# Transposing Q with the DMA crossbar instead of TensorE in a fused attention and FFN kernel

## The chip, the cores and the metric

The kernel runs on one core of one Trainium2 chip. The metric is the device time of one execution in microseconds. A profile is one such execution recorded by the hardware profiler; its times count from the start of its span. Engines are called as the profile calls them: PE is TensorE (PEld its weight loads), DVE is VectorE, ACT is ScalarE, POOL is GpSimd and SP is SyncE, whose queue issues DMAs.

## What is computed

Sliding-window causal attention over 8 batches, 8 heads, 576 positions and 64 values per head, followed by a multiplicative feed-forward block on the 4608 tokens:

```python
scores = scale * np.matmul(q, k.transpose(0, 1, 3, 2))
rel = pos[:, None] - pos[None, :]
mask = (rel >= 0) & (rel < 64)
scores = np.where(mask, scores, -1000000000.0)
attn = np.exp(scores - np.max(scores, axis=-1, keepdims=True))
attn = attn / (np.sum(attn, axis=-1, keepdims=True) + 1e-09)
x = np.matmul(attn, v)              # then heads side by side: 4608 x 512
a, b = x @ w1, x @ w2               # 512 x 1024 each
h = a * b @ w3                      # 1024 x 1024
out = h @ w_out                     # 1024 x 512
```

Inputs and output are float32; the kernel computes in fp16 with float32 sums.

## The kernel before

**Attention.** Work goes in 48 steps `d`, six for each batch: three segments of queries (`SEGS`, 192 queries each) times two pairs of head pairs. Two heads share the 128 partitions (64 each, called `a`), and `j` counts the four pairs of heads. `scores(d)` multiplies a block of 128 keys (stationary, `kT`) with up to 128 queries (moving, `qT`), so that keys lie on the partitions of `s_ps`, eight matmuls in a step (line 278). One exponential on ScalarE (line 282) takes the step from PSUM to the fp16 tile `pt`, and GpSimd masks it in place with `affine_select` (lines 290 and 292; two for a step with two full blocks, four for the first segment, whose blocks have 128 and 64 queries). `values(d)` multiplies with V, whose added columns of ones give the sums; ScalarE takes logarithms and the exponential of their negative (lines 320 to 323), and DVE writes the normalised result to `xT` (lines 326 and 327).

**K and Q on their way.** `load_qk` brings a batch of K or Q from memory in two DMAs of 576 KB into a tile `stage` (four buffers). Partition p holds 18 consecutive positions of one head pair (`TP, TI = 32, 18`). `cast_qk` makes fp16 of it in `k16` or `q16` (one buffer each), mostly on GpSimd (line 214). `transposes` turns it on TensorE, 18 transposes of 128x128 in three groups of six into PSUM (line 253), and three copies (line 257: K all on DVE, Q two on DVE and one on ScalarE) put it into `kT` or `qT` in the order of positions.

**The feed-forward block.** w3 and w_out are multiplied together once, at the start. `ffn_ab(g, fc)` makes one of eight blocks of the product for 512 tokens with 16 matmuls (or eight per half; line 395), `ffn_o(g, t)` one of four blocks of 128 rows of the output with eight (line 408), and `store` sends it off from the SP queue.

**Order.** The order on each engine is that of the program text; nothing is scheduled automatically. Batches 0 and 1 are written out by hand, up to about 80 us. From batch 2 on, `tick(u)` counts twelve ticks to a batch: an even tick starts `scores(u // 2)`, an odd one does `values` of the step before, so that the values of step d come three ticks after its scores. The table `late` (line 335) tells in which tick of a batch the loads, casts and transposes for the coming batches are put. The list `slots` (line 608) deals out the feed-forward pieces between ticks. A waiting instruction holds up all behind it on its engine, or, on SP, all DMAs behind it. In tick 24, the first of batch 2, the masks of step 12 are followed on GpSimd by a cast of Q of batch 3, in tick 25 by the second cast, and in tick 26 by the masks of step 13.

Of the kernel before, what the change touches and what calls it, by code (L numbers as in the profile page):

```python
# [8 lines left out]
FP32 = mybir.dt.float32  # L9
FP16 = mybir.dt.float16  # L10
I32 = mybir.dt.int32
ALU = mybir.AluOpType
AF = mybir.ActivationFunctionType
PSUM = bass.MemoryType.PSUM

P = 128
SHIFT = 4.0
# [127 lines left out]
def kernel(  # L145
# [11 lines left out]
    nc = tc.nc  # L157
    B, H, S, D = q.shape
# [3 lines left out]
    scale = 1.0 / (D ** 0.5)  # L162
    NJ = H // 2
    TP, TI = 32, 18
    GT = 512
    NG = N // GT
    RING = 4 * S
# [12 lines left out]
    const = fast.enter_context(tc.tile_pool(name="const", bufs=1))  # L180
    sb = fast.enter_context(tc.tile_pool(name="sb", bufs=2))
    ps_t = fast.enter_context(tc.tile_pool(name="ps_t", bufs=1, space=PSUM))
    ps_s = fast.enter_context(tc.tile_pool(name="ps_s", bufs=1, space=PSUM))
# [3 lines left out]
    pool_cp = nc.gpsimd.tensor_copy  # L187
# [9 lines left out]

    raws, k16s, q16s = {}, {}, {}

    def load_qk(b, which, gate=None):  # L200
        src = k if which == "k" else q
        t = sb.tile([P, 2, TI * D], FP32, name="stage", bufs=4)
        if gate is not None:
            gate(t[:, 0, 0:1], 0.0)
        for hh in range(2):
            nc.sync.dma_start(out=t[:, hh], in_=src[b, hh:H:2].rearrange("j (p r) d -> p j (r d)", r=TI))
        raws[which, b] = t

    def cast_qk(b, which, hh, cp):
        t = raws[which, b]  # L210
        if hh == 0:
            (k16s if which == "k" else q16s)[b] = sb.tile([P, TI, P], FP16, name=which + "16", bufs=1)
        t16 = (k16s if which == "k" else q16s)[b]
        cp(t16[:, :, hh * D:hh * D + D], t[:, hh].rearrange("p (i d) -> p i d", d=D))

    def cast_third(b, which, c, cp):
        t = raws[which, b]
# [9 lines left out]
    def load_v(b, *blocks):  # L227

        vh = v_heads(b)
        for c in blocks:  # L230
            lo = D if c == 4 else 0
            s0 = VBLK[c] + lo
            nc.gpsimd.dma_start(out=vh[lo:P, c], in_=v[b, :, s0:s0 + P - lo, :].rearrange("h s d -> s h d"))  # L233

    def copy_v(b, c):
        vh = v_heads(b)
        dve_cp(vh[0:D, c], vh[D:P, c - 1])
        if c == 1:
            dve_cp(vh[D:P, 1], vh[0:D, 2])


    kTs, qTs = {}, {}

    def transposes(b, which, *cs, into=None, cps=None):

        t16, dst = (k16s, kTs) if which == "k" else (q16s, qTs)
        if cs[0] == 0:
            dst[b] = sb.tile([P, NJ, S], FP16, name=which + "T")
        if into is None:
            into = [ps_t.tile([P, 6, P], FP16, name="tp")]  # L250
        for c, tp in zip(cs, into):
            for i in range(6):
                nc.tensor.transpose(tp[:, i, :], t16[b][:, 6 * c + i, :], ident16)  # L253
        if cps is None:
            cps = [dve_cp if which == "k" or c != 1 else act_cp for c in cs]
        for c, tp, cp in zip(cs, into, cps):
            cp(dst[b].rearrange("q j (p i) -> q j p i", i=TI)[:, :, :, 6 * c:6 * c + 6],  # L257
               tp.rearrange("q i (p j) -> q j p i", p=TP))


    MASKS = [[(0, 1, 128, 0, 0), (128, 1, 64, 64, 0)]] + 2 * [[(0, 2, 128, 64, -64)]]
    probs, lns = {}, {}

    def scores(d):

        b, r = divmod(d, 6)
        si, jp = divmod(r, 2)
        kT, qT = kTs[b], qTs[b]
        seg = SEGS[si]
        w = sum(blk[2] for blk in seg)  # L270
        s_ps = ps_s.tile([P, 2, 2, 256], FP32, name="s_ps")
        for jj in range(2):
            j = 2 * jp + jj
            c0 = 0
            for (k0, q0, n, _) in seg:
                for a in range(2):
                    half = slice(a * D, a * D + D)
                    nc.tensor.matmul(s_ps[:, a, jj, c0:c0 + n], kT[half, j, k0:k0 + P], qT[half, j, q0:q0 + n],  # L278
                                     start=True, stop=True, skip_group_check=True)
                c0 += n  # L280
        pt = sb.tile([P, 2, 2, 256], FP16, name="pt", bufs=3)
        nc.scalar.activation(pt[:, :, :, 0:w], s_ps[:, :, :, 0:w], AF.Exp, bias=-SHIFT, scale=scale)  # L282

        rows = pt.rearrange("k a j n -> k (a j) n")
        for (lo, nb, n, off, step) in MASKS[si]:
            sl = rows[:, :, lo:lo + nb * n]
            pat = [[0, 4], [step, nb], [1, n]]
            if nb == 1:
                pat = [[0, 4], [1, n]]
            nc.gpsimd.affine_select(out=sl, in_=sl, pattern=pat, compare_op=ALU.is_ge,  # L290
                                    fill=0.0, base=off, channel_multiplier=-1)
            nc.gpsimd.affine_select(out=sl, in_=sl, pattern=[[-s, m] for s, m in pat], compare_op=ALU.is_ge,  # L292
                                    fill=0.0, base=63 - off, channel_multiplier=1)
        probs[d] = pt
# [34 lines left out]
    def keep_sums(n):  # L329
# [2 lines left out]
        nc.sync.dma_start(out=lnsum[2 * n:2 * n + 2, :], in_=y[0:P:D].rearrange("a j n -> a (j n)"))  # L332


    late = {0: [("t", 1, "k", 0), ("cast", 1, "q", 0)], 1: [("cast", 1, "q", 1)],
            2: [("t", 1, "k", 1), ("load", 2, "k")], 4: [("t", 1, "k", 2), ("v", 1, 0, 2, 3)],
            5: [("load", 2, "q")], 6: [("t", 1, "q", 0), ("v", 1, 4, 5)], 7: [("cast", 2, "k", 0)],
            8: [("t", 1, "q", 1), ("copy", 1, 4)], 9: [("copy", 1, 1), ("cast", 2, "k", 1)], 10: [("t", 1, "q", 2)]}

    def event(b, kind, ahead, *a):  # L340
        if b + ahead >= B:
            return
        if kind == "load":
            load_qk(b + ahead, *a)
        elif kind == "cast":
            cast_qk(b + ahead, *a, pool_cp)
        elif kind == "t":
            transposes(b + ahead, *a)
        elif kind == "v":
            load_v(b + ahead, *a)  # L350
        else:
            copy_v(b + ahead, *a)
# [25 lines left out]

    def ffn_ab(g, fc, nf=1, lo=0, hi=GT):

        if g not in abs_:
            abs_[g] = sb.tile([P, 8, GT], FP16, name="ab", bufs=3)
        ab = abs_[g]
        n = hi - lo
        a_ps = ps_f.tile([P, GT], FP32, name="f_ps")
        b_ps = ps_f.tile([P, GT], FP32, name="f_ps")
        x0 = (g * GT + lo) % RING
        cuts = [(0, n)] if x0 + n <= RING else [(0, RING - x0), (RING - x0, n)]
        for w, d in ((w1_sb, a_ps), (w2_sb, b_ps)):
            first = True  # L390
            for f in range(nf):
                for dc in range(4):
                    for c0, c1 in cuts:
                        xc = (x0 + c0) % RING
                        nc.tensor.matmul(d[:, f * n + c0:f * n + c1], w[:, dc, (fc + f) * P:(fc + f + 1) * P],  # L395
                                         xT[:, dc, xc:xc + c1 - c0], start=first, stop=(dc == 3),
                                         skip_group_check=True)
                        first = False
        a_sb = sb.tile([P, GT], FP32, name="a_sb", bufs=3)
        act_cp(a_sb[:, 0:nf * n], a_ps[:, 0:nf * n])  # L400
        nc.vector.tensor_tensor(ab[:, fc:fc + nf, lo:hi], b_ps[:, 0:nf * n].rearrange("p (f n) -> p f n", f=nf),  # L401
                                a_sb[:, 0:nf * n].rearrange("p (f n) -> p f n", f=nf), ALU.mult)
# [11 lines left out]
    def store():  # L414
        while stores:
            r0, o_sb = stores.pop()
            nc.sync.dma_start(out=out[r0:r0 + P, :], in_=o_sb)
# [39 lines left out]
    rows = 2 * 3 * B  # L457
# [48 lines left out]
    def spare(pool, name):  # L506

        t = pool.tile([P, 2, 1024], FP16, name=name)
        return [t[:, i, 0:768].rearrange("p (i n) -> p i n", i=6) for i in range(2)]
# [67 lines left out]
    for d in range(6, 11):  # L577
        values(d)
        if d < 10:
            scores(d + 2)  # L580
        for _ in range(2 if d in (6, 8) else 1):
            steps.pop(0)()
            store()
        if d == 6:
            load_v(2, 4, 5)
            copy_v(1, 4)
            load_qk(3, "k")
        else:
            which, hh = [("k", 0), ("k", 1), ("q", 0), ("q", 1)][d - 7]
            cast_qk(2, which, hh, pool_cp)  # L590
    transposes(2, "k", 0, 1, into=spare(ps_s, "s_ps"))
    values(11)
    transposes(2, "k", 2)
# [1 line left out]
        cast_qk(3, "k", hh, pool_cp)  # L595
    ffn_o(0, 3)
    store()
    transposes(2, "q", 0, 1, into=spare(ps_s, "s_ps"))
    transposes(2, "q", 2)
    copy_v(2, 1)  # L600
    copy_v(2, 4)
    load_qk(3, "q")
# [6 lines left out]
    for g in range(1, NG):  # L609
        part = [lambda g=g, fc=fc: ffn_ab(g, fc) for fc in range(8)] + \  # L610
               [lambda g=g, t=t: ffn_o(g, t) for t in range(4)]
        lo = need[g]
        hi = need[g + 1] if g + 1 < NG else NU
        for i, w in enumerate(part):
            ahead = (LAG + 1) * (min(1, (i + 1) / 4) if g == 1 else 1)
# [55 lines left out]
```

## Time and profile before

Three runs took 295.75, 296.19 and 296.27 us; the median is 296.19. The profiled execution has a span of 294.3 us.

| engine | busy us | share of the span | what it does most |
|---|---|---|---|
| PE | 274.1 | 93% | feed-forward matmuls, 134.1 + 67.1 us |
| DVE | 185.4 | 63% | products and copies out of PSUM |
| POOL | 180.8 | 61% | masks, 52.1 + 52.4 us; casts of K and Q, 28.3 us |
| ACT | 168.4 | 57% | exponentials 45.5 us, copies 41.7 us |

The groups of the page that touch the change, each with its number of instructions, its busy time and the mean duration of one:

| group | count | busy us | mean ns |
|---|---|---|---|
| score matmuls, 128 columns (line 278) | 320 | 17.8 | 219 |
| score matmuls, 64 columns | 64 | 4.4 | 189 |
| transposes of Q into `tp` (line 253) | 108 | 9.1 | 220 |
| copies of transposed Q on DVE, from `tp` (line 257) | 13 | 12.3 | 949 |
| copies of transposed Q on ACT, from `tp` | 5 | 4.0 | 808 |
| exponential of 1024 elements (line 282) | 32 | 32.6 | 1018 |
| exponential of 768 elements | 16 | 13.0 | 810 |
| casts of Q on POOL (line 214) | 13 | 14.6 | 1146 |

Matmuls overlap each other, so the mean of a matmul is longer than the time that it adds to TensorE's stream; that is read from the distance between starts of groups in the timeline. In the chain of work that ended last, PE has 76% of the span.

### The profile page before, as it was taken

Reading aid. Unit: us, or ns where it says so; the run is one execution under the profiler, and the core shown is the slowest. Engines: PE = TensorE matmul, PEld = TensorE weight load, DVE = VectorE, ACT = ScalarE, POOL = GpSimd, SP = SyncE. Lnnn points to the kernel's source line nnn. Section 1 sums busy time; section 2 is a strip of 40 time slices with the busy share of each in tenths; the row PEclk is TensorE's granted clock in tenths of the full one; section 3 lists DMA queues with packets and bytes.
Section 4 is the critical chain, followed back from the end, with each engine's and each line's share of the span. In section 5 each row is a group of like instructions: output and inputs, shape, how many; then the busy total and the mean of one; then the engine's idle time right before and its main releaser. Section 6 shows DMA issues by size and latency. Waiting matters only on the chain.

```text
span 294.3 us, 5925 instructions
## 1 busy us (share of the span) xinstructions
PE 274.1 (93%) x2254; PEld 152.9 (52%) x2254; DVE 185.4 (63%) x289; ACT 168.4 (57%) x281; POOL 180.8 (61%) x214
## 2 busy tenths in 40 slices
PE   7758889898799999999999999999999999999992
PEld 7544555444455555555555787555555445444440
DVE  0715688465787667687777866677867555554541
ACT  2513774676458647766686565487568866642300
POOL 8835995478749856696869463786595344402200
PEclk9999999999999999999999999999999999999998
DMA  6999999990277939094929470950094021012012
GB/s 231 219 181 201 265 278 212 373 131 36 74 266 264 72 110 321 39 85 143 322 20 100 136 295 2 155 73 1 20 171 40 0 74 72 0 38 109 0 57 95
DMA packets 51665, 38.85 MB, mean 132 GB/s; under 512 B 38784, under 2 KB 41856, under 8 KB 51632
## 3 DMA queue, kind: packets, MB, share of 16 engines
q0 software_dynamic: 41744, 9.96, 36.2%
q1 hardware_dynamic: 9888, 28.46, 26.6%
q8 instruction: 19, 0.31, 0.4%
q14 instruction: 14, 0.11, 0.1%
HBM read 38.80 MB, written 9.44 MB: 164 GB/s over the span
## 4 chain that ended last, share of the span: by engine, by line
PE 76%; DVE 6%; ACT 5%; DMA 4%; issue 3%; POOL 3%; POOLq 0%; DVEq 0%; ACTq 0%
PE f_ps L395 38%; PE f_ps L408 19%; PE o_ps L311 7%; PE tp L253 5%; DMA ab<-in_moe_w_dram 4%; PE s_ps L278 4%; DVE xT L327 2%; PE f_ps L454 2%; ACT ln_s L321 2%; ACT r L323 2%; POOL v L488 2%; DVE kT L257 1%; DVE xT L326 1%; ACT ln_s L320 1%; ACT pt L282 1%
## 5 line engine op out<-in xcount | busy, mean ns | idle before, releaser
L395 PE MATMUL f_ps<-xT,w_sb 128*128 128x512 f16 (+1 forms) x640 | 134.1, 358 | 0.0
L290 POOL TENSOR_SCALAR_AFFINE_SELECT pt<-pt 128x512 f16<-128x512 f16 (+1 forms) x64 | 52.1, 814 | 69.0 <-ACT pt L282 68.9
L395 PEld LDWEIGHTS <-w_sb 128*128 128x128 f16 x640 | 59.7, 98 | 50.7 <-issue 0.5
L408 PE MATMUL f_ps<-wc_sb,ab 128*128 128x512 f16 x288 | 67.1, 379 | 0.1
L401 DVE TENSOR_TENSOR ab<-f_ps,a_sb 128x512 f16<-128x512 f32 x72 | 49.8, 692 | 18.4 <-PE f_ps L395 15.8
L326 DVE TENSOR_TENSOR xT<-o_ps,r 64x384 f16<-64x384 f32 x48 | 26.4, 550 | 53.8 <-ACT r L323 53.6
L282 ACT ACTIVATE pt<-s_ps 128x1024 f16<-128x1024 f32 (+1 forms) x48 | 45.5, 949 | 18.0 <-PE s_ps L278 16.5
L400 ACT COPY a_sb<-f_ps 128x512 f32<-128x512 f32 x72 | 41.7, 579 | 24.8 <-PE f_ps L395 23.9
L292 POOL TENSOR_SCALAR_AFFINE_SELECT pt<-pt 128x512 f16<-128x512 f16 (+1 forms) x64 | 52.4, 819 | 4.4
L320 ACT ACTIVATE ln_s<-o_ps 64x384 f32<-64x384 f32 x48 | 23.4, 487 | 53.4 <-PE o_ps L311 53.3
L408 PEld LDWEIGHTS <-ab 128*128 128x128 f16 x288 | 26.9, 98 | 28.8 <-DVE ab L401 0.6
L233 POOL DMA_DIRECT2D v<-in_v_dram x40 | 33.9, 854 | 5.9 <-DMA ab<-in_moe_w_out_dram 4.1
L311 PE MATMUL o_ps<-pt,v 128*128 128x128 f16 (+1 forms) x384 | 27.9, 215 | 5.9 <-DVE xT L327 4.0
L311 PEld LDWEIGHTS <-v 128*128 128x128 f16 x384 | 23.5, 98 | 18.2 <-issue 3.5
L410 DVE COPY t2k<-f_ps 128x512 f32<-128x512 f32 x36 | 24.7, 690 | 11.6 <-PE f_ps L408 11.1
L327 DVE TENSOR_TENSOR xT<-o_ps,r 64x384 f16<-64x384 f32 x48 | 26.9, 561 | 0.6
L323 ACT ACTIVATE r<-ln_s 128x384 f32<-128x384 f32 x48 | 25.1, 523 | 1.5
L321 ACT ACTIVATE ln_s<-o_ps 64x384 f32<-64x384 f32 x48 | 23.1, 482 | 0.5
L278 PEld LDWEIGHTS <-kT 64*128 64x128 f16 x384 | 10.5, 94 | 16.5 <-issue 14.8
L278 PE MATMUL s_ps<-qT,kT 64*128 64x128 f16 (+1 forms) x384 | 18.2, 214 | 0.3 <-ACT pt L282 0.2
L257 DVE COPY kT<-tp 128x768 f16<-128x768 f16 x17 | 16.2, 952 | 0.1
L454 PE MATMUL f_ps<-ab,t2k 128*128 128x512 f16 x64 | 15.0, 379 | 0.4 <-DVE t2k L448 0.3
(59 smaller groups left out, 179.8 us busy)
## 6 DMA issues: line engine op xcount, KB each, us to landing
stage<-in_k_dram SPq DMA_DIRECT2D x16, 576.0 KB
stage<-in_q_dram SPq DMA_DIRECT2D x16, 576.0 KB
out_dram<-t2k SPq DMA_DIRECT2D x36, 256.0 KB
v<-in_v_dram POOLq DMA_DIRECT2D x32, 128.0 KB, 4.7
w_sb<-in_moe_w_dram POOLq DMA_DIRECT2D x4, 512.0 KB, 9.5
ab<-in_moe_w_out_dram POOLq DMA_DIRECT2D x1, 1024.0 KB, 10.6
ab<-in_moe_w_dram POOLq DMA_DIRECT2D x2, 512.0 KB, 12.6
xT<-in_moe_w_dram POOLq DMA_DIRECT2D x2, 512.0 KB, 16.2
```

The costliest lines, as they stand in the source:

```text
L233: nc.gpsimd.dma_start(out=vh[lo:P, c], in_=v[b, :, s0:s0 + P - lo, :].rearrange("h s d -> s h d"))
L278: nc.tensor.matmul(s_ps[:, a, jj, c0:c0 + n], kT[half, j, k0:k0 + P], qT[half, j, q0:q0 + n], start=True, stop=True, skip_group_check=True)
L282: nc.scalar.activation(pt[:, :, :, 0:w], s_ps[:, :, :, 0:w], AF.Exp, bias=-SHIFT, scale=scale)
L290: nc.gpsimd.affine_select(out=sl, in_=sl, pattern=pat, compare_op=ALU.is_ge, fill=0.0, base=off, channel_multiplier=-1)
L292: nc.gpsimd.affine_select(out=sl, in_=sl, pattern=[[-s, m] for s, m in pat], compare_op=ALU.is_ge, fill=0.0, base=63 - off, channel_multip ...
L311: nc.tensor.matmul(o_ps[:, jj, o0:o0 + n], v16[:, si * 2 + bi, j0 + jj, a * D:a * D + P], pt[:, a, jj, c0:c0 + n], start=first, stop=(bi = ...
L323: nc.scalar.activation(r, y, AF.Exp, scale=-1.0)
L327: nc.vector.tensor_tensor(xs[D:P], o_ps[D:P, :, 192:384], r[D:P], ALU.mult)
L395: nc.tensor.matmul(d[:, f * n + c0:f * n + c1], w[:, dc, (fc + f) * P:(fc + f + 1) * P], xT[:, dc, xc:xc + c1 - c0], start=first, stop=(dc ...
L400: act_cp(a_sb[:, 0:nf * n], a_ps[:, 0:nf * n])
L401: nc.vector.tensor_tensor(ab[:, fc:fc + nf, lo:hi], b_ps[:, 0:nf * n].rearrange("p (f n) -> p f n", f=nf), a_sb[:, 0:nf * n].rearrange("p ...
L408: nc.tensor.matmul(o_ps, ab[:, fc, t * P:t * P + P], wc_sb[:, fc, :], start=(fc == 0), stop=(fc == 7))
```

## The change

From batch 2 on (`FIRST = 2`) Q isn't transposed on TensorE any more. SP issues one DMA transpose for each batch (`turn`), which goes from `q16` in SBUF to a tile `q_tr` in SBUF, with no PSUM and no copy in between. It is meant to take the transposes off TensorE and the copies off DVE and ScalarE.

A partition now holds 16 consecutive positions (`QI`), so a batch's tile has 512 of the 576 positions. The last 64 of all batches and heads are loaded together as one more tile, `"last"`, cast and transposed once into `qlast`. `q_tr` has the order (position within 16, group of 16): the score matmuls read it as it lies, in runs of eight groups, and their result in PSUM has the same order. The exponential reads PSUM with a stride and writes `pt` in the order of positions, so all that follows is as it was. In the first segment it becomes two instructions. A block that crosses position 512 takes two matmuls in place of one. `stage` has three buffers instead of four.

```diff
+    def turn(b):
+        tr = qlast if b == "last" else sb.tile([P, QI, P], FP16, name="q_tr", bufs=2)
+        nc.sync.dma_start_transpose(tr, q16s[b].rearrange("q i n -> q (i n)"))
+        qTs[b] = tr
...
-        t = sb.tile([P, 2, TI * D], FP32, name="stage", bufs=4)
+        t = sb.tile([P, 2, TI * D], FP32, name="stage", bufs=3)
...
+            elif b == "last":
+                rows = q.rearrange("b (j e) s d -> e (b j) s d", e=2)[hh, :, TP * QI:S]
+                nc.sync.dma_start(out=t[:, hh, 0:QI * D], in_=rows.rearrange("j (p r) d -> j p (r d)", r=QI))
+            else:
+                nc.sync.dma_start(out=t[:, hh, 0:QI * D],
+                                  in_=q[b, hh:H:2, 0:TP * QI].rearrange("j (p r) d -> j p (r d)", r=QI))
...
+                    o = s_ps[:, a, jj, c0:c0 + n].rearrange("k (i p) -> k i p", i=QI)
+                    p0, p1 = q0 // QI, (q0 + n) // QI
+                    mid = min(p1, TP)
+                    nc.tensor.matmul(o[:, :, 0:mid - p0], kT[half, j, k0:k0 + P], qT[half, :, TP * j + p0:TP * j + mid],
                                      start=True, stop=True, skip_group_check=True)
+                    if p1 > TP:
+                        c = 16 * b + 4 * j
+                        nc.tensor.matmul(o[:, :, mid - p0:p1 - p0], kT[half, j, k0:k0 + P],
+                                         qlast[half, :, c:c + p1 - TP], start=True, stop=True, skip_group_check=True)
...
+            for (lo, nb, n, _, _) in MASKS[si]:
+                x, y = src[:, :, lo:lo + nb * n], rows[:, :, lo:lo + nb * n]
+                if nb > 1:
+                    x, y = (t.rearrange("k f (c n) -> k (f c) n", c=nb) for t in (x, y))
+                nc.scalar.activation(y.rearrange("k f (p i) -> k f p i", i=QI), x.rearrange("k f (i p) -> k f p i", i=QI),
+                                     AF.Exp, bias=-SHIFT, scale=scale)
...
-    late = {0: [("t", 1, "k", 0), ("cast", 1, "q", 0)], 1: [("cast", 1, "q", 1)],
+    late = {0: [("t", 1, "k", 0), ("cast", 1, "q", 0)], 1: [("cast", 1, "q", 1), ("turn", 1)],
             2: [("t", 1, "k", 1), ("load", 2, "k")], 4: [("t", 1, "k", 2), ("v", 1, 0, 2, 3)],
-            5: [("load", 2, "q")], 6: [("t", 1, "q", 0), ("v", 1, 4, 5)], 7: [("cast", 2, "k", 0)],
-            8: [("t", 1, "q", 1), ("copy", 1, 4)], 9: [("copy", 1, 1), ("cast", 2, "k", 1)], 10: [("t", 1, "q", 2)]}
+            5: [("load", 2, "q")], 6: [("v", 1, 4, 5)], 7: [("cast", 2, "k", 0)],
+            8: [("copy", 1, 4)], 9: [("copy", 1, 1), ("cast", 2, "k", 1)]}
...
+        if d == 9:
+            load_qk("last", "q")
+    turn(2)
     transposes(2, "k", 0, 1, into=spare(ps_s, "s_ps"))
...
-    transposes(2, "q", 0, 1, into=spare(ps_s, "s_ps"))
-    transposes(2, "q", 2)
+    for hh in range(2):
+        cast_qk("last", "q", hh, pool_cp)
+    turn("last")
     copy_v(2, 1)
     copy_v(2, 4)
     load_qk(3, "q")
```

## Prediction before the run

> **What bounds the kernel now.** I read the page's busy shares first, then the stages, then TensorE in order of time, because the shares alone do not say in which stretch TensorE is the limit.
>
> ```profile
> PE 274.1 (93%) x2254; PEld 152.9 (52%) x2254; DVE 185.4 (63%) x289; ACT 168.4 (57%) x281; POOL 180.8 (61%) x214
> ```
>
> No engine but TensorE is near full. The table of stages shows where that is exact (columns: stage, length, then busy time of PE, weight loads, DVE, ACT, POOL with instruction counts, clock, DMA share, GB/s):
>
> ```profile
> 92.00:256.00 164.00, 164.00 (x1342) 91.03 (x1340) 114.58 (x178) 110.64 (x187) 109.11 (x128) 1.00 0.52 104
> ...
> 77.00:92.00 15.00, 13.35 (x125) 7.37 (x123) 12.55 (x20) 8.47 (x15) 9.44 (x14) 1.00 0.68 247
> ```
>
> From 92 to 256 us TensorE never pauses, so there every nanosecond taken from its stream is a nanosecond of the span. From 77 to 92 us, where batch 2 starts, it is idle for 1.65 us, and other engines set the pace. TensorE in order of time (start, length, the tile, the count):
>
> ```profile
> 93.60 0.40 PE L278 MATMUL s_ps<-qT,kT 64*128 64x128 f16 x8
> 93.93 0.51 PE L253 MATMUL tp<-ident,q 128*128 128x128 f16 x6
> 94.28 1.89 PE L395 MATMUL f_ps<-xT,w_sb 128*128 128x512 f16 x8
> ```
>
> The distance between starts is what a group costs, since lengths overlap: eight score matmuls of 128 columns cost 0.33 us, or 41 ns each, and six Q transposes cost 0.35 us, or 58 ns each.
>
> GpSimd at the start of batch 2, in order of time; the bracket is the idle time before and who ended it:
>
> ```profile
> 74.85 2.23 POOL L214 CAST q<-stage 128x1152 f16<-128x1152 f32 x2
> 77.45 2.24 POOL L214 CAST k<-stage 128x1152 f16<-128x1152 f32 x2 [0.37 <-PE tp L253]
> 84.60 0.64 POOL L290 TENSOR_SCALAR_AFFINE_SELECT pt<-pt 128x512 f16<-128x512 f16 x1 [4.91 <-ACT pt L282]
> ...
> 86.75 2.23 POOL L214 CAST q<-stage 128x1152 f16<-128x1152 f32 x2
> 88.93 0.64 POOL L290 TENSOR_SCALAR_AFFINE_SELECT pt<-pt 128x512 f16<-128x512 f16 x1
> ```
>
> The masks of step 12 are followed by the two casts of Q of batch 3, and only then by the masks of step 13, which end at 91.1 us. The value matmuls of step 13 start at 91.44 us, just behind them. This order decides my forecast.
>
> **What the skill says.** The Trainium skill, "VectorE: DVE Perf Modes", section "The three transpose paths", gives 1309 ns for one 128x128 transpose through the crossbar and 390 ns on TensorE. In this trace a TensorE transpose in a row costs 58 ns, so its figures are for one alone. "DMA: Bandwidth & Descriptors", section "Latency and other measured facts", gives 261 GB/s as the effective rate of a DMA transpose; the trace of before has none. "SBUF — State Buffer", section "Door 1: The DMA port swizzle", says that SBUF has lines of 16 bytes and gives full bandwidth with two or more hits on a line. The new score matmuls read runs of eight fp16 (16 bytes), or four where a run is cut; no strided moving operand is in the trace.
>
> **The change part by part.**
>
> *TensorE transposes removed.* Batches 3 to 7 lose 18 each in the full stretch: 5 x 18 x 58 ns = 5.2 us, all on the path. The 18 of batch 2 (78.94 to 81.27 us) go as well. Without them the first FFN group of batch 2 waits only for its activations, whose last product ends at 79.90 us. Six of its eight first matmuls follow (0.216 us each, 1.73 us for eight), so the scores of step 12 could start at 81.2 us; before they start at 83.27.
>
> *More score matmuls.* In the last segment each block is cut at query 512: 4 more matmuls in 2 of a batch's 6 steps, 48 in all. A group of four 128- and four 64-column matmuls costs 0.28 us (83.27 to 83.55), so 64 columns cost (0.28 - 4 x 0.041)/4 = 29 ns. Two of these for one of 41 adds 17 ns, 48 times: 0.8 us on the path.
>
> *The strided read by TensorE.* By the line rule it is free; at the other end each score matmul takes twice as long, 12 groups x 0.28 + 24 x 0.33 = 11.3 us. I take nothing and keep that end as a case.
>
> *The exponential.* ScalarE reads PSUM with a stride. The trace has a near row: its copy of transposed Q reads 768 elements from PSUM with a stride of 128 and takes 808 ns, and the contiguous exponential over 768 takes 810. So the stride is free. The split of the first segment into 512 and 256 elements adds one fixed cost: 810 for 768 and 1018 for 1024 give 0.81 ns per element and 0.19 us fixed, for 12 steps 2.3 us, against six copies of 0.81 us that go. It hides behind TensorE, as do the DVE's twelve removed copies.
>
> *Loads, casts, buffers.* Loads of Q shrink by a ninth and casts from 1147 to about 1.02 us; two casts and one load are added for the last 64 rows. One stage buffer less is free in the loop: at most two loads are live at once. All hide, except at the start of batch 2.
>
> *The crossbar transpose.* T is the time from issue to landing of one 512 KB transpose. For its data I use the nearest row: software-queue packets of 239 bytes on average (9.96 MB in 41744) take 36.2% of 16 x 294.3 us, or 41 ns each. 2048 packets of 256 bytes over 16 engines are 128 x 41 ns = 5.2 us. For the fixed part: loads of V of 128 KB land in 4.7 us and of 64 KB in 3.3, which leaves 1.9 at zero size. T = 7.1 us. The skill's two prices bound it: 512 KB at 261 GB/s is 2.0 + 1.9 = 3.9 us; sixteen times 1309 ns is 20.9 + 1.9 = 22.8 us.
>
> In the loop a transpose is issued in tick 1 of a batch and wanted eleven ticks later (a batch takes some 28 us): hidden. The queue of SyncE behind it holds the next K load, six ticks ahead of its cast, and stores with four buffers: hidden for T near 7.
>
> At the start of batch 2 it isn't hidden. SyncE issues the first transpose after the store that leaves at 77.04 + 0.33 us and after the cast ending at 77.08: 77.4. It lands at 77.4 + T = 84.5, and the scores of step 12 wait. The buffer q16 is single, so GpSimd's two casts of the last rows must wait until the transpose has read it; they end at 84.5 + 2.05 = 86.5. The second transpose lands at 86.5 + 7.1 = 93.6. The load of Q of batch 3 is now behind it on the same queue; I add 1.5 us after that landing (0 if side by side; about 3 if its 1.05 MB follow at 350 GB/s, a rate that the trace shows around 85 us). GpSimd, after the masks of step 12, meets the casts of batch 3, which need both that load and q16: 95.1 + 2.05 = 97.2. Queued behind are the masks of step 13 (2.2 us), ending at 99.4, and for them wait the values of step 13 on TensorE. Before they ended at 91.1: 8.3 us lost. Later casts and transposes run late too, but their consumers are four or more ticks away, so I count no second stall.
>
> Sum: 296.2 + 8.3 - 5.2 + 0.8 = 300.1 us. With T open it is 285.9 + 2T, equal to before at T = 5.15.
>
> **The rivals.**
>
> *Fast crossbar, faster than before.* At T = 3.9 the sum gives 293.7 us; if the load of Q also lands beside the transpose instead of behind it, 1.5 less, 292.2. For it: the skill's rate, and DMA engines at a share of 0.29 from 78 to 80 us. Against it: 256-byte rows cost 41 ns here, whatever the rate of long packets.
>
> *Slow crossbar.* At T = 13 the sum is 311.9, at 22.8 us 331.5, and SyncE's queue would then delay K loads in the loop too. For it: the price of a lone transpose. Against it: sixteen of them can overlap over 16 engines.
>
> *Slow strided matmuls.* 300.1 + 11.3 = 311.4 us, since TensorE is the bound; against it the 16-byte lines.
>
> *ScalarE becomes the bound* if strided PSUM reads double 36 exponentials (some 34 us more on 168): it stays below TensorE's 274, with local waits of perhaps 3 us: 303. The copy at 808 ns speaks against it.
>
> **How the numbers follow.** My forecast with T between 5.3 and 12: 0.40, and ScalarE's case 0.03. Fast crossbar, with T below 5: 0.37. Near break-even: 0.05. Slow crossbar or slow matmuls: 0.15. Hence faster 0.37, same 0.05, slower 0.58. The range runs from 293.0, leaving out 0.05 at the fast end, to 312.0, which takes in T = 13 and the doubled matmuls and leaves out some 0.1.
>
> **What would show it.** In the profile after: no transposes of Q past 78 us and each full batch 1 us shorter on TensorE; score groups of 0.28 to 0.33 us, or longer where striding costs; exponentials of 1018 ns still; a wait of TensorE for the transposed Q before step 12, of GpSimd's casts for the transposes, and of the values of step 13 for the masks. I am wrong if the two transposes land within some 5 us each, or if GpSimd is not held by q16 between 82 and 95 us.

## The result, and the profile after

The changed kernel takes 345.74 us (median of four runs, 342.54 to 349.85) against 296.18 before: a ratio of 1.164, with a 95% interval of 1.156 to 1.173. The ratio compares fast runs alone and so leaves out the one of 349.85 us. The forecast had the direction, slower, but 300.1 us and a range that ended at 312.0.

The page's busy shares after the change, and the granted clock of TensorE in 40 slices of the span, in tenths:

```profile
PE 280.4 (82%) x2194; PEld 153.5 (45%) x2194; DVE 172.1 (50%) x277; ACT 164.8 (48%) x287; POOL 181.8 (53%) x216
...
PEclk9899999999956987999589978999699999999998
```

TensorE has 60 instructions less and 6.3 us more of busy time, and its granted clock is low in five places. The chain of work that ended last says what it waited for, first in the kernel before, then after the change:

```profile
PE 76%; DVE 6%; ACT 5%; DMA 4%; issue 3%; POOL 3%; POOLq 0%; DVEq 0%; ACTq 0%
```

```profile
PE 47%; DMA 28%; POOL 8%; DVE 5%; ACT 5%; issue 4%; SPq 0%; POOLq 0%; ACTq 0%; DVEq 0%
PE f_ps L439 26%; DMA v<-in_v_dram 19%; PE f_ps L452 9%; PE o_ps L353 5%; DMA stage<-in_q_dram 4%; DMA ab<-in_moe_w_dram 3%; POOL pt L332 2%; POOL v L245 2%; PE s_ps L307 2%; DVE xT L369 2%; DMA q_tr<-q 2%; PE f_ps L498 2%; PE tp L274 2%; POOL v L532 2%; ACT ln_s L363 1%
```

DMA has risen from 4% to 28%, and neither of its two large entries is the new transpose (2%): they are loads of V (19%) and of Q (4%). TensorE in order of time at its first stall in batch 2, and at the first one in the loop:

```profile
83.65 0.35 PE L307 MATMUL s_ps<-q_tr,kT 64*128 64x128 f16 x8 [2.27 <-DMA q_tr<-q]
...
104.58 0.27 PE L353 MATMUL o_ps<-pt,v 128*128 128x128 f16 x1 [13.14 <-POOL pt L334]
105.44 0.69 PE L353 MATMUL o_ps<-pt,v 128*128 128x64 f16 x7 [0.59 <-POOL pt L334]
105.94 3.56 PE L439 MATMUL f_ps<-xT,w_sb 128*128 128x512 f16 x8
109.43 0.40 PE L307 MATMUL s_ps<-q_tr,kT 64*128 64x128 f16 x8
...
130.30 3.31 PE L452 MATMUL f_ps<-wc_sb,ab 128*128 128x512 f16 x8 [8.34 <-DVE t2k L454]
```

The wait for the transposed Q is 2.27 us. The values of step 13 then wait 13.14 us for their masks. Later, in the loop, there are waits of 8.34 (shown), 8.17, 7.19 and 5.72 us. After a long wait, eight feed-forward matmuls take 3.5 us instead of 1.73 (105.94 to 109.43): TensorE runs at half clock (0.50 from 106 to 109 us). GpSimd shows what held the masks of step 13:

```profile
83.66 2.03 POOL L226 CAST q<-stage 128x1024 f16<-128x1024 f32 x2 [3.99 <-DMA q_tr<-q]
...
97.18 1.04 POOL L226 CAST q<-stage 128x1024 f16<-128x1024 f32 x1 [9.35 <-DMA stage<-in_q_dram]
102.20 1.04 POOL L226 CAST q<-stage 128x1024 f16<-128x1024 f32 x1 [3.98 <-DMA stage<-in_q_dram]
```

The first line is the forecast wait for `q16`. The other two wait for the load of Q of batch 3, whose halves land at 97.2 and 102.2 us although it was issued between 87.7 and 89.2. The list of waits of all engines, longest in total first, names the loop's stalls (total, times, longest):

```profile
DVE v L249 <- DMA v<-in_v_dram: 40.9, 4, 13.0
...
PE o_ps L353 <- DVE xT L369: 19.0, 10, 8.2
PE o_ps L353 <- POOL pt L334: 14.6, 4, 13.1
```

In each of four batches DVE stands at the copy of a V block until V has landed; the products behind it, and TensorE behind those, stand too. The last number of these two lines is the median time of a load of V from issue to landing, before and after:

```profile
v<-in_v_dram POOLq DMA_DIRECT2D x32, 128.0 KB, 4.7
```

```profile
v<-in_v_dram POOLq DMA_DIRECT2D x32, 128.0 KB, 13.8
```

SyncE never waited for a free `stage` buffer in the loop, so the buffer that the change takes away is not what holds the loads up.

The sum over the profiles: waits of TensorE after 79 us 45.8 us against 1.6 before, so +44.3; half-clock groups after the five long waits, each against the same groups at full clock, 1.9 + 1.4 + 2.7 + 1.6 + 2.4 = 10.0; transposes gone, 108 x 58 ns = 6.3, so -6.3. That makes +48.0 of the 49.0 us between the spans (343.3 and 294.3).

**The load of Q.** Two stages in which Q was being loaded, from 84 us in the kernel before (with a load of K between two of Q) and from 92 us after; the last two columns are the mean busy share of the 16 DMA engines and GB/s:

```profile
84.00:92.00 8.00, 7.62 (x72) 4.00 (x69) 5.69 (x9) 5.41 (x10) 7.13 (x11) 1.00 1.00 383
```

```profile
92.00:100.00 8.00, 0.00 (x0) 0.00 (x0) 1.36 (x2) 0.00 (x0) 1.04 (x1) 0.73 0.26 103
```

After, the load of Q has the DMA engines to itself and keeps them busy for a mean of 0.26, as much as four of sixteen would. The diff moved the head pair, of which there are four, to the outside of the source (`-> j p (r d)` in place of `-> p j (r d)`). The Trainium skill, "DMA: Bandwidth & Descriptors", section "Why a DMA increments its semaphore by 16 and not by 1", says that a DMA is spread over the largest number of engines, at most 16, that divides the outermost counts of both sides: 16 for 32 groups, 4 for four head pairs. The share of 0.26 agrees. The forecast did not look at this.

### The profile page after: what moved, and what is told of

Its sections match the earlier page's. It is cut to its first block, busy times and chain, and to the rows that moved or that the text cites. A ratio compares the mean times of both kernels' runs of the same rounds, so it can differ in the third digit from the quotient of the medians.

```text
span 343.3 us, 5809 instructions
## 1 busy us (share of the span) xinstructions
PE 280.4 (82%) x2194; PEld 153.5 (45%) x2194; DVE 172.1 (50%) x277; ACT 164.8 (48%) x287; POOL 181.8 (53%) x216
## 4 chain that ended last, share of the span: by engine, by line
PE 47%; DMA 28%; POOL 8%; DVE 5%; ACT 5%; issue 4%; SPq 0%; POOLq 0%; ACTq 0%; DVEq 0%
PE f_ps L439 26%; DMA v<-in_v_dram 19%; PE f_ps L452 9%; PE o_ps L353 5%; DMA stage<-in_q_dram 4%; DMA ab<-in_moe_w_dram 3%; POOL pt L332 2%; POOL v L245 2%; PE s_ps L307 2%; DVE xT L369 2%; DMA q_tr<-q 2%; PE f_ps L498 2%; PE tp L274 2%; POOL v L532 2%; ACT ln_s L363 1%
## 5 line engine op out<-in xcount | busy, mean ns | idle before, releaser
L439 PE MATMUL f_ps<-xT,w_sb 128*128 128x512 f16 (+1 forms) x640 | 140.9, 370 | 6.1 <-DVE ab L445 5.7
L439 PEld LDWEIGHTS <-w_sb 128*128 128x128 f16 x640 | 61.6, 101 | 61.2 <-issue 12.2
L452 PE MATMUL f_ps<-wc_sb,ab 128*128 128x512 f16 x288 | 68.6, 385 | 8.5 <-DVE t2k L454 8.3
L353 PE MATMUL o_ps<-pt,v 128*128 128x128 f16 (+1 forms) x384 | 29.6, 221 | 34.6 <-DVE xT L369 19.0
L353 PEld LDWEIGHTS <-v 128*128 128x128 f16 x384 | 24.7, 101 | 48.0 <-issue 35.3
L324 ACT ACTIVATE pt<-s_ps 128x1024 f16<-128x1024 f32 (+2 forms) x48 | 35.0, 755 | 22.0 <-PE s_ps L307 13.5
L249 DVE COPY v<-v 64x512 f16<-64x512 f16 x16 | 5.6, 349 | 41.2 <-DMA v<-in_v_dram 40.9
L226 POOL CAST q<-stage 128x1024 f16<-128x1024 f32 (+1 forms) x15 | 15.4, 1048 | 17.3 <-DMA stage<-in_q_dram 13.3
L307 PEld LDWEIGHTS <-kT 64*128 64x128 f16 x288 | 8.0, 94 | 17.4 <-issue 14.6
```

The costliest lines, as they stand in the source:

```text
L324: nc.scalar.activation(y.rearrange("k f (p i) -> k f p i", i=QI), x.rearrange("k f (i p) -> k f p i", i=QI), AF.Exp, bias=-SHIFT, scale=scale)
L353: nc.tensor.matmul(o_ps[:, jj, o0:o0 + n], v16[:, si * 2 + bi, j0 + jj, a * D:a * D + P], pt[:, a, jj, c0:c0 + n], start=first, stop=(bi = ...
L452: nc.tensor.matmul(o_ps, ab[:, fc, t * P:t * P + P], wc_sb[:, fc, :], start=(fc == 0), stop=(fc == 7))
```

## The experiments

**Theory A:** the load of Q on four DMA engines is the cause; what shares them, V above all, lands late. **Theory B:** the crossbar transposes themselves hold up the other transfers.

**Load cut into 32 rows.** The changed kernel, each load in DMAs of 32 partitions:

```diff
-                nc.sync.dma_start(out=t[:, hh, 0:QI * D],
-                                  in_=q[b, hh:H:2, 0:TP * QI].rearrange("j (p r) d -> j p (r d)", r=QI))
+                for j in range(NJ):
+                    nc.sync.dma_start(out=t[TP * j:TP * j + TP, hh, 0:QI * D],
+                                      in_=q[b, hh + 2 * j, 0:TP * QI].rearrange("(p r) d -> p (r d)", r=QI))
```

> The changed kernel with each load of Q from batch 2 on cut into four DMAs of 32 partitions per half (one for each head pair), so that the outermost count of the source is 32 and no longer 4; layout and everything else as changed. Theory A (a load with an outer count of 4 runs on 4 of the 16 DMA engines, at some 100 GB/s, and what shares those engines with it lands late): the waits of DVE for V and of POOL for Q go away, only the start of batch 2 costs, and by the sum on record with T near 6.2 us the time is about 298 us (293 to 301). Theory B (the crossbar transposes themselves hold up other transfers): still above 335 us.

Measured: 305.06 us, ratio 1.029 (1.027 to 1.032). 40.7 of the 49.6 us are gone with the load alone, so B falls as the main cause, though the time is 4 us above A's range too. TensorE in this run:

```profile
83.04 0.35 PE L308 MATMUL s_ps<-q_tr,kT 64*128 64x128 f16 x8 [1.68 <-DVE ab L446]
...
97.49 0.27 PE L354 MATMUL o_ps<-pt,v 128*128 128x128 f16 x1 [6.65 <-POOL pt L335]
```

This is the forecast start of batch 2: scores at 83.0 (forecast 84.5), masks of step 13 ending at 98.3 (forecast 99.4). Only the first wait is named differently: here it ends with a product on DVE, in the changed kernel with the transposed Q. The rest is a half-clock stretch after the wait and short waits for V in batches 2 to 4; V lands in 8.3 us.

**The groups outermost again, in two DMAs:**

```diff
+                                  in_=q[b, hh:H:2, 0:TP * QI].rearrange("j (p r) d -> p j (r d)", r=QI))
...
-                    nc.tensor.matmul(o[:, :, 0:mid - p0], kT[half, j, k0:k0 + P], qT[half, :, TP * j + p0:TP * j + mid],
+                    nc.tensor.matmul(o[:, :, 0:mid - p0], kT[half, j, k0:k0 + P], qT.rearrange("n i (p j) -> n j i p", j=NJ)[half, j, :, p0:mid],
```

> The changed kernel with the load of Q written with its 32 groups outermost again (two DMAs per batch, as before), so that a head pair's columns lie four apart in the transposed tile and the score matmuls read runs of eight with a step of four elements. Theory A: as with the cut loads, about 298 us (293 to 301) if the stride of eight bytes costs TensorE nothing, up to 11 us more if it doubles the score matmuls. Theory B: above 335 us.

Measured: 304.67 us, ratio 1.025 (1.018 to 1.032). The same load in as many DMAs as in the changed kernel, but with 32 outside, mends it as well; so neither the number of DMAs nor the shorter rows of Q are the cause. V lands in 6.0 us, and TensorE has no wait after 99 us. From there on it loses to the stride of 8 bytes: score groups take 0.42 to 0.54 us instead of 0.27 to 0.33, some 6 us in 36 groups. So the stride that the changed kernel chose is free, and this one isn't.

**The load alone, transposes on TensorE:**

```diff
+            if which == "q" and b >= 2:
+                nc.sync.dma_start(out=t[:, hh], in_=src[b, hh:H:2].rearrange("j (p r) d -> j p (r d)", r=TI))
...
+            order = "q i (j p) -> q j p i" if which == "q" and b >= 2 else "q i (p j) -> q j p i"
```

> The kernel before (transposes on TensorE) with nothing changed but the order of partitions in the loads of Q from batch 2 on: head pair outermost, an outer count of 4, and the copies after the transposes read in the matching order. Theory A: the load alone makes it slow, 330 to 350 us. Theory B: 296 us within 2.

Measured: 314.25 us, ratio 1.060 (1.056 to 1.063). The slow load costs 18 us by itself, but A's 330 to 350 is missed. Most of it is one wait, before the values of step 13, and the half clock after it; no later wait is longer than 2.2 us:

```profile
102.01 0.27 PE L315 MATMUL o_ps<-pt,v 128*128 128x128 f16 x1 [10.85 <-POOL pt L296]
```

**No crossbar, the slow load kept.** This kernel leaves the transposes out, and its score matmuls read a tile of zeros:

```diff
-        tr = qlast if b == "last" else sb.tile([P, QI, P], FP16, name="q_tr", bufs=2)
-        nc.sync.dma_start_transpose(tr, q16s[b].rearrange("q i n -> q (i n)"))
-        qTs[b] = tr
+        qTs[b] = qlast
...
+    nc.gpsimd.memset(qlast, 0.0)
```

> The changed kernel with its seven crossbar transposes left out (the score matmuls read a tile of zeros instead of Q, so the attention isn't the reference's); the loads of Q keep their outer count of 4. Theory A: still slow, 325 to 346 us. Theory B: at most 300 us.

Measured: 304.21 us, ratio 1.028 (1.023 to 1.032). Both theories are wrong here: the time lies above B's 300 us and far below A's 325. Again there is one long wait, and none above 0.9 us after it:

```profile
100.49 0.27 PE L351 MATMUL o_ps<-pt,v 128*128 128x128 f16 x1 [11.47 <-POOL pt L332]
```

Slow load alone: 18 us with the transposes on TensorE, 8 us without any (108 of them are 6.3 us less work). Crossbar alone, with cut loads: 9 us. Both: 49.6 us. So the two act together, and the traces say where: each alone makes TensorE wait at the start of batch 2, for 5.6 to 11.5 us, and leaves no wait above 2.2 us in the loop; the four waits of 5.7 to 8.3 us in the loop are there only with both. (The runs without the slow load and the one without the crossbar have three `stage` buffers too, so that these do not make the waits.) SyncE's queue in the loop and GpSimd's issue of V show one way in which they act together. First batch 3 of the changed kernel, then batch 4 without the crossbar:

```profile
141.03 1.81 SPq L262 DMA_TRANSPOSE q_tr<-q  x1
142.89 1.80 SPq L212 DMA_DIRECT2D stage<-in_k_dram  x2
...
145.40 1.17 SPq L217 DMA_DIRECT2D stage<-in_q_dram  x2
...
148.65 2.66 POOL L245 DMA_DIRECT2D v<-in_v_dram  x3
```

```profile
150.07 1.17 SPq L217 DMA_DIRECT2D stage<-in_q_dram  x2
...
161.32 2.65 POOL L245 DMA_DIRECT2D v<-in_v_dram  x3
```

Without the crossbar SyncE runs ahead, and the load of Q has 11.3 us before V begins, about what 1.05 MB take at 103 GB/s (in the kernel before it had 10.8). With the crossbar SyncE stands before the transpose until GpSimd has cast Q, and V comes 3.3 us after the load.

**The transpose behind the loads; the start of batch 2 mended; both.** The first cut below moves the transpose, the second mends the start, and the third kernel has both:

```diff
-    late = {0: [("t", 1, "k", 0), ("cast", 1, "q", 0)], 1: [("cast", 1, "q", 1), ("turn", 1)],
+    late = {0: [("t", 1, "k", 0), ("cast", 1, "q", 0)], 1: [("cast", 1, "q", 1)],
             2: [("t", 1, "k", 1), ("load", 2, "k")], 4: [("t", 1, "k", 2), ("v", 1, 0, 2, 3)],
-            5: [("load", 2, "q")], 6: [("v", 1, 4, 5)], 7: [("cast", 2, "k", 0)],
+            5: [("load", 2, "q"), ("turn", 1)], 6: [("v", 1, 4, 5)], 7: [("cast", 2, "k", 0)],
```

```diff
-            (k16s if which == "k" else q16s)[b] = sb.tile([P, n, P], FP16, name=which + "16", bufs=1)
+            (k16s if which == "k" else q16s)[b] = sb.tile([P, n, P], FP16, name=which + "16", bufs=2 if which == "q" else 1)
...
     turn(2)
+    load_qk(3, "q")
...
-    load_qk(3, "q")
```

> The changed kernel with one move: the crossbar transpose of a batch goes from tick 1 to tick 5, behind the load of Q in SyncE's queue; the loads of Q keep their outer count of 4. Theory A (in the loop SyncE stands before the transpose until GpSimd has cast Q, so that the K and Q loads behind it start some 8 us later than before, on top of the V loads; the slow load and the late start are both needed for the stalls): the waits for V in the loop go away, the start of batch 2 stays as it is, 304 to 311 us. Theory B (the transposes' own traffic, or the slow load wherever it lies, holds up V): above 328 us.

> The changed kernel with only the start of batch 2 mended: two buffers for q16, and the load of Q of batch 3 right behind the first transpose instead of behind the second. Theory A: the 13 us wait before the values of step 13 goes away, the four waits for V in the loop (29 us and the half-clock stretches after them) stay: 322 to 332 us. If the loop's waits were a consequence of the late start: 291 to 300 us.

> Both mends together (transpose behind the loads in the loop; two q16 buffers and the earlier load at the start), the loads of Q still with an outer count of 4. Theory A: no long wait is left and TensorE's 5.2 us less show: 290 to 295 us. If the load on few engines costs by itself: above 298 us.

Measured: 324.05 us (ratio 1.091, 1.081 to 1.101), 339.78 (1.148, 1.139 to 1.157) and 321.27 (1.085, 1.079 to 1.090). All three miss A's numbers, and the first lies below B's 328 too: the order of the queue gives 22 us, the start 6 us, both together 24, and 25 us over the kernel before remain, as was expected if the load on few engines costs by itself. With the order alone TensorE's waits in the loop fall to 4.37, 2.83, 1.30 and 0.84 us, so the order accounts for 20 of their 29 us. But in that kernel the transpose also stands behind the slow load:

```profile
135.49 1.18 SPq L217 DMA_DIRECT2D stage<-in_q_dram  x2
139.74 11.00 SPq L262 DMA_TRANSPOSE q_tr<-q  x1
```

Its issue takes 11.00 us where the changed kernel's takes 1.8, so it slips into the time of V, which is issued from 147.37 us on. Mending the start also helped less than expected: the slow load of Q, issued at 81.8, still reaches its casts at 91.0 and 96.0 us.

**Both mends with cut loads:** the edits above and

```diff
+                for j in range(2 * hh, 2 * hh + 2):
+                    nc.sync.dma_start(out=t[TP * j:TP * j + TP, :, 0:QI * D],
+                                      in_=q[b, 2 * j:2 * j + 2, 0:TP * QI].rearrange("e (p r) d -> p e (r d)", r=QI))
```

> As the one with both mends, and each load of Q cut into four DMAs of 32 partitions over both halves, so that the outer count is 32. Theory A: 290 to 293 us, within 2 us of the one with both mends, since the slow load no longer lies on top of V.

Measured: 299.09 us, ratio 1.009 (1.007 to 1.012). The cut is worth 22 us here too, so the slow load still costs with the queue's order and the start mended; A had expected less than 2 us here, and fails.

**The crossbar from batch 3 on**, so that no transpose lies in the start of batch 2; with cut loads, then with the load as changed:

```diff
-    FIRST = 2
+    FIRST = 3
...
+        if u == 30:
+            load_qk("last", "q")
+        if u == 34:
+            for hh in range(2):
+                cast_qk("last", "q", hh, pool_cp)
+            turn("last")
```

> The crossbar from batch 3 on instead of 2, so that the start of batch 2 is as in the kernel before; loads of Q cut into four DMAs of 32 partitions, transposes behind the loads in the loop (tick 5), two q16 buffers, the last rows loaded, cast and transposed in ticks 30 and 34. Theory A: the start costs nothing, TensorE's 5.2 us less show but for short waits for V: 291 to 294 us, faster than before. Theory B (the transposes' traffic keeps V late in every batch): 296 us or more.

> The same, but with the loads of Q left as changed (outer count of 4). Theory A: four DMA engines then have 256 KB of Q each per batch (10.5 us at the 25 GB/s per engine seen) on top of their share of K, V, stores and the transpose, nearly a batch's 28 us, so V lands late in the loop although the start is as before: 303 to 318 us. Theory B (only the start and the place of the transposes matter): within 3 us of the run with cut loads.

Measured: 297.27 us (ratio 1.002, 0.9998 to 1.004) and 323.01 (1.090, 1.087 to 1.092). Two kernels that differ only in the cut of the load are 26 us apart, and the second is 5 us above A's range. There the start isn't as before after all: the casts of batch 3 still wait for the slow load, and the values of step 13 wait 10.11 us. The better kernel is level with the kernel before, and not at A's 291 to 294: short waits for masks and V (1.34 + 0.64, 1.29 and 0.85 us) and one half-clock group (1.8 us) take what TensorE gained.

**Last, the order of transfers**, in the better of these two kernels: V in ticks 3 and 4, the transpose in tick 6, the load of Q of batch 3 earlier; beside it, the kernel before with the two moves of loads alone:

```diff
-            2: [("t", 1, "k", 1), ("load", 2, "k")], 4: [("t", 1, "k", 2), ("v", 1, 0, 2, 3)],
-            5: [("load", 2, "q"), ("turn", 1)], 6: [("v", 1, 4, 5)], 7: [("cast", 2, "k", 0)],
+            2: [("t", 1, "k", 1), ("load", 2, "k")], 3: [("v", 1, 0, 2, 3)], 4: [("t", 1, "k", 2), ("v", 1, 4, 5)],
+            5: [("load", 2, "q")], 6: [("turn", 1)], 7: [("cast", 2, "k", 0)],
...
+        if d == 10:
+            load_qk(3, "q")
```

> As the crossbar from batch 3 on with cut loads, and three moves in the order of transfers: V of the next batch in ticks 3 and 4 instead of 4 and 6, the transpose in tick 6, behind it, and the load of Q of batch 3 ahead of the last K transposes of batch 2. Theory A (what is left is V and Q arriving late): no wait of TensorE over 1 us after 80 us, 291 to 294 us. Theory B (the crossbar's traffic costs more than TensorE gains): 296 us or more.

> The kernel before (all transposes on TensorE) with only the two moves of loads: V in ticks 3 and 4, the load of Q of batch 3 earlier. It tells what of a gain is due to the order of transfers and not to the crossbar. TensorE has no wait to lose there after 92 us: 295.5 to 297 us.

Measured: 296.21 us, ratio 0.999 (0.997 to 1.001), and 296.59, ratio 1.000 (0.999 to 1.001). Neither can be told from the kernel before, and A's 291 to 294 us is missed again. In the first, one wait is left after 93 us:

```profile
138.47 0.61 PE L354 MATMUL o_ps<-pt,v 128*128 128x128 f16 x8 [2.53 <-DVE xT L370]
```

Its profiled span is 293.1 us against 294.3, but that execution was the fastest of 14 (the spans of all go from 293.1 to 296.7). From the values of step 13 on, which are these in the kernel before and in this one, it takes 200.7 us against 202.9:

```profile
91.44 0.50 PE L311 MATMUL o_ps<-pt,v 128*128 128x128 f16 x8 [0.38 <-DVE xT L327]
```

```profile
92.41 0.50 PE L354 MATMUL o_ps<-pt,v 128*128 128x128 f16 x8 [0.38 <-DVE xT L370]
```

The 1 us before them isn't the crossbar's: the run with the order alone has it too (92.57 us). So in this execution the crossbar keeps 2.2 of the 5.2 us that TensorE gave up, the wait of 2.53 us takes about the rest, and nothing of it shows in the timed runs.

## Why the prediction was right or wrong

- **TensorE transposes removed: right.** In undisturbed stretches each group of six that is gone makes TensorE's stream 0.33 us shorter (from one group of scores to the next 4.34 us, from 149.41 to 153.75, where it was 4.67), and nothing takes its place.
- **More score matmuls: too high.** A group with cut blocks takes 0.33 to 0.34 us, as one without. The 0.8 us did not show.
- **Strided read and exponential: right.** Score groups stay at 0.27 and 0.33 us; the exponential of 1024 elements takes 1024 ns (1018 before), the split one 597 + 378. The line rule of the Trainium skill, "SBUF — State Buffer", section "Door 1: The DMA port swizzle", holds for the runs of eight in a row. It does not hold for the step of four elements that the second experiment tried: that has two hits on a line and still costs 0.15 to 0.21 us a group.
- **T: right in size.** Forecast 7.1 us; the first transpose took 6.2 from issue (77.46) to the scores it released (83.65), and the one of the last rows 4.3 in a later run, where the DMA engines were idle before it. The chain through `q16`, casts and masks was right too: the run with cut loads follows it within 1.5 us, and its 305.06 us is slower than before without any slow load. So the direction was no luck, though the two signs of being wrong that the forecast named did not point to what went wrong.
- **"I add 1.5 us after that landing": wrong, and the first of the two steps that broke the sum.** The traffic of the second transpose ends near 90 us, and the second half of Q lands at 102.2: some 12 us. The values of step 13 start 13.1 us later than before (104.58 against 91.44), where the forecast had 8.3. The load's size was counted and a rate of the kernel before (350 GB/s) was put to it, though the diff changed its access pattern. Its rate is 103 GB/s; its second half alone, 512 KB, takes 5.0 us.
- **"I count no second stall": wrong, and the larger one.** Waits of 8.34, 8.17, 7.19 and 5.72 us follow in the loop. The step looked at consumers of K and Q. The V loads, on another queue but the same DMA engines, were not in it, nor was SyncE, which now stood at the transpose: it issued the load of Q 9.7 us after a batch's first scores (145.40 and 135.72), where it had been 2.1 us (140.90 and 138.77).
- **Half clock: missing from the sum.** Some 10 us after five waits. With 29.4 us of waits in the loop and 4.8 us more at the start, that is 44 of the 45.6 us between forecast and measurement.
- **The rivals.** None was the case that came. "Slow crossbar" came nearest in size, with 331.5 us, but for the wrong cause: the transpose is not slow. The rivals asked what each new instruction costs and not what a rewritten old one does.

What stays open is how the load and the transposes add up to more than their parts. One part is shown, the queue order (22 us when the transpose is moved). For the rest there is an estimate from the rates of these traces, if Q lies on four engines and the other transfers on all sixteen: on the four engines a batch has 256 KB of Q, at 26 GB/s each 10 us; 144 packets of V at 41 ns, 5.9; the transpose's 128 packets, some 3; K and stores at 24 GB/s each, some 3 each. That is 25 us in a batch of 28, which leaves little room for transfers that come late. No run measured a single engine, so this is argued and not shown.

## What to carry to other kernels

When a load's access pattern is turned, count what lies outermost on both sides before anything else: with 4 instead of 32 the load of Q ran at 103 GB/s here, where loads of Q and K had run at 383, and its victims were loads on another queue. A DMA that waits for a cast, put into an in-order queue, takes from all loads behind it the lead that they had. And time taken from the bounding engine is only kept if nothing else becomes late: here 5.2 us of TensorE work went, and the best arrangement kept 2.2 us of it in one profile and nothing in the timed runs.

## What the runs showed of the hardware

**Crossbar.** A crossbar transpose of 512 KB from SBUF to SBUF took 4.3 us from issue to landing where the DMA engines were idle before it, 6.7 us beside a store and loads of V, and 7.4 us behind a load of Q cut in four. In the changed kernel its issue took 1.8 to 4.1 us of SyncE's time. Behind a load with 4 outermost it took 8.8 to 15.7 us, and behind cut loads 3.8 to 9.1.

**Clock.** TensorE's clock fell to half in the five long waits of the changed kernel (5.7 to 13.1 us) and stayed there through the next 3 to 6 us of matmuls. The Trainium skill, "TensorE: Matmul & The Clock Gate", section "Part 1: The HAM clock gate", gives windows of about 3.4 us for both, and in the changed kernel the slices agree (0.50 from 96 to 104 us, after TensorE had stopped at 91.4). Other runs fell earlier than that. In the kernel with both mends TensorE stopped at 81.3, and after a wait of only 3.09 us it ran at half clock:

```profile
84.41 0.51 PE L307 MATMUL s_ps<-q_tr,kT 64*128 64x128 f16 x8 [3.09 <-DMA q_tr<-q]
...
85.46 3.62 PE L439 MATMUL f_ps<-xT,w_sb 128*128 128x512 f16 x8
```

With cut loads as well, two waits of 1.31 and 0.64 us were followed by eight matmuls in 3.5 us, while 2.27 us in the changed kernel and 2.53 in the last one cost no clock. In the profiles of the changed kernel and of the experiments, every wait of TensorE of 3 us or more after 79 us was followed by half clock; after shorter ones it was sometimes so and sometimes not.
